# Clustered attention before a mixture of experts: the first head pair prepared on its own, v's scale taken per batch on ScalarE, and four transposes issued from ScalarE's queue

## The chip, the cores and the metric

The kernel runs on one core of a Trainium2 chip. The metric is the device time of one execution in microseconds. The kernel before took 1464.55 us (median of 3 runs, 1462.3 to 1464.61). The profile is that of one further execution, of 1462.42 us, whose span from the first to the last instruction is 1460.6 us.

## The reference

Only the attention part is touched by the change; the two dense stages behind it use its result.

```python
# q, k, v: (2, 8, 768, 64); centroids: (8, 16, 64)
q_assign = argmax(q_n . c_n);  k_assign = argmax(k_n . c_n)      # 16 clusters per head
mask = q_assign[:, :, :, None] == k_assign[:, :, None, :]
scores = where(mask, scale * q @ k.T, -1e9)
attn = softmax(scores)                                           # minus the row's maximum
x = attn @ v                                                     # (2, 8, 768, 64) -> (1536, 512)
h = x @ w_in;  x = (h * clip(h + 3, 0, 6) / 6) @ w_out            # d_ff 2048
# then 8 experts, each relu(x @ w1[e]) @ w2[e], weighted by a normalised gate
```

## The kernel before

The 16 heads of the two batches are worked as 8 pairs of heads, pair p holding heads 2p and 2p+1. A head has 6 tiles of 128 rows, so there are 96 units (head i, tile c), numbered g = 0 to 95. All engines run in the order in which the program writes the instructions; a wait on one of them holds up everything behind it on the same engine.

**Preparing a pair** (`prep_tasks`). ScalarE sums the squares of q and k (`squares`, L491). TensorE and VectorE turn the sums into power-of-two scales (`scale0` to `scale2`). Then `chain` splits q and k into two halves of 16 bits each: `hi` on ScalarE (L549), `lo` (L553) and `dup` (L560) on VectorE, and a DMA transpose gives qB and kB (L563). `sims` (L573, L574) compares them with the centroids on TensorE, five VectorE steps (`arg_max` to `arg_oh`) make the cluster codes, `rows` writes the codes beside the halves on ScalarE (L602, L603), and two more DMA transposes give qA and kA (L607). The last tasks are `vhi` (ScalarE, L530) and `vlo` (VectorE, L535), which split v with v's scale, and `abs1` to `abs3`. Pair 0 goes through `chain` in two parts, h0 and h1, one for each head, so that its first unit can start on the first half; the other pairs go through it in one (pair 1: `both1`).

**A unit.** `max_unit` multiplies 128 rows of q with all k (L680) and VectorE takes the maximum of each row (L683); it runs LEAD = 8 units ahead, so the loop starts at g = -8. `max_rows` writes the six maxima of a head into qA's rows and transposes them once more (L694). `s_mm` makes the scores on TensorE (L729, L733) and ScalarE takes the exponential E (L737). `e_split` splits E into Eh (ScalarE, L745) and El (L747 on VectorE for some units, L750 on GpSimd for the others). `pv_mm`, LAG = 4 units later, multiplies with v (L765). `evac_tasks` divides by the sums.

**v's scale.** Before, `scan_v` takes the largest modulus of v in four VectorE reductions of half a batch each (L836), and one scale serves both batches (`scale_v0`, `scale_v1`).

**What sets the order.** Ahead of the loop the order is written out by `go(...)`. Inside it, tasks are hung on units with `at(g, f)`: PLAN2 for pair 2, PLANV for the scans, v's scale and the last tasks of pairs 0 and 1. All DMAs, the transposes among them, are issued from SyncE's queue, in order. First weights of the dense stages are scanned and decoded between the units (L350, L181).

In the text "h0" and "h1" are pair 0's two halves, and E_4 is the exponential of unit g = 4.

Of the kernel before, what the change touches and what calls it, by code (L numbers as in the profile page):

```python
# [8 lines left out]
F32 = mybir.dt.float32  # L9
# [10 lines left out]
P = 128  # L20
NJ = 6
# [11 lines left out]
def attention_moe_kernel(  # L33
# [446 lines left out]
    def prep_tasks(p, parts=None):  # L480
# [46 lines left out]

        def vhi():
            vn = d["vn"] = ap3.tile([P, 2 * NJ, 130], F16, tag="vn", name=f"vn{p}")
            nc.scalar.activation(vn[:, :, 0:D], vr, AF.Copy, scale=sv[0][:, 0:1])  # L530
            nc.gpsimd.memset(vn[:, :, D:D + 1], 1.0)

        def vlo():
            vn = d["vn"]
            nc.vector.scalar_tensor_tensor(  # L535
                out=vn[:, :, D + 1:2 * D + 1], in0=vr, scalar=sv[0][:, 0:1], in1=vn[:, :, 0:D],
                op0=ALU.mult, op1=ALU.subtract)

        def chain(tr):
# [60 lines left out]
            def rows():  # L600
                oh = x["oh"]
                nc.scalar.activation(qa[:, tr, D:D + C], oh[:, 0:n], AF.Copy, scale=MASK)  # L602
                nc.scalar.activation(ka[:, tr, D:D + C], oh[:, n:], AF.Copy, scale=MASK, bias=-MASK)  # L603
                for nm, nat in (("q", qa), ("k", ka)):
                    if tr.start == 0:
                        d[nm + "A"] = ap2.tile([P, 2 * NJ, P], F16, tag=f"{nm}A", name=f"{nm}A{p}")
                    nc.sync.dma_start_transpose(  # L607
                        out=d[nm + "A"][:, tr], in_=nat[:, tr].rearrange("p a b -> p (a b)"))

            two = [lambda g=g, nm=nm: g(nm) for g in (hi, lo, dup) for nm in "qk"]  # L610
# [171 lines left out]
    def evac_tasks(i):  # L782
        p, hh = divmod(i, 2)
        b, hp = divmod(p, H // 2)
        ps = pvt.pop(i)
        if hh == 0:
            xn[p] = [ap2.tile([P, NJ, P], F16, tag=f"xn{z}", name=f"xn{z}_{p}") for z in range(2)]
        xs = xn[p]
        r = small.tile([P, NJ], F32, tag="x_r", name=f"x_r{i}")
        xf = ap2.tile([P, NJ, D], F32, tag="x_f", name=f"x_f{i}", bufs=1)  # L790
        xh, xl = (x[:, :, D * hh:D * hh + D] for x in xs)

        def e0():
# [83 lines left out]
    sv = [None, None]

    vred = []

    def scale_v0():
        nc.vector.tensor_reduce(pad[:, 0:1], vmx, axis=AX.X, op=ALU.max)
        vred.append(ps_v.tile([P, 2 * P], F32, tag="v", name="red_v"))
        red_rows(vred[0][:, 0:P])

    def scale_v1():
        to_all(red_max(vred[0][:, 0:P], "v"), vred[0][:, P:P + 1])
        sv[:] = scale_of(vred[0][:, P:P + 1], 1, 1, "v", const)
# [41 lines left out]
    def at(g, f):  # L930
        tasks.setdefault(g, []).append(f)
# [16 lines left out]

    for n, f in zip((2, 7, 9, 13, 14, 18, 19, 25, 26, 33, 35, 36, 47, 48), wscan):
# [877 lines left out]
```

## Time and profile before

| | |
|---|---|
| median of 3 runs | 1464.55 us (1462.3 to 1464.61) |
| the profiled execution / its span | 1462.42 us / 1460.6 us |
| TensorE busy | 1353.3 us, 93% |
| VectorE busy | 1200.2 us, 82% |
| ScalarE busy | 921.3 us, 63% |
| GpSimd busy | 795.6 us, 54% |

The attention part ends at about 300 us of the span; from there on TensorE is busy without a gap. The change lies in its first 70 us, where no engine is busy throughout and the engines wait for each other in turn. The way to read it is therefore not by busy shares but in order of time, engine by engine: which instruction waits there, for whom, and what stands behind it.

### The profile page before, as it was taken

The numbers are of one execution on the slowest core, as the hardware profiler recorded it, in microseconds if no ns is written. First come the engines' busy times: TensorE is split into PE (matmuls) and PEld (weight loads), VectorE is DVE, ScalarE is ACT, GpSimd is POOL, SyncE is SP. The second block draws the span as 40 slices with busy tenths as digits, with TensorE's granted clock in tenths as the row PEclk, the third lists the DMA queues.
The fourth block names the chain that finished last, engine by engine and source line by source line (L and its number), as shares of the span: only waits on it lengthen the run. The fifth ranks groups of instructions, "written<-read, shape, count | busy, mean of one in ns | idle before, by whom it ended". The sixth has DMA issues, their size and how long they took to land.

```text
span 1460.6 us, 31114 instructions
## 1 busy us (share of the span) xinstructions
PE 1353.3 (93%) x12334; PEld 1058.4 (72%) x12334; DVE 1200.2 (82%) x2111; ACT 921.3 (63%) x1723; POOL 795.6 (54%) x831
## 2 busy tenths in 40 slices
PE   2788777899999996989999999999999999999998
PEld 1456555644444445878888888888888888888887
DVE  8889998777775668788988988988988988988954
ACT  2679877867374456566767666666666656657642
POOL 1357866735034556365666566566566556656631
PEclk9889989999999998999999999999999999999999
DMA  8576644241312101101111111111111111111001
GB/s 223 127 170 115 140 99 68 53 127 59 126 65 59 45 17 31 31 32 31 45 31 46 44 31 46 44 31 45 44 32 45 45 31 46 45 31 46 8 31 51
DMA packets 150194, 88.92 MB, mean 61 GB/s; under 512 B 83488, under 2 KB 145952, under 8 KB 150048
## 3 DMA queue, kind: packets, MB, share of 16 engines
q1 hardware_dynamic: 150048, 86.94, 22.8%
q8 instruction: 96, 1.57, 0.5%
q14 instruction: 50, 0.41, 0.1%
HBM read 64.01 MB, written 3.15 MB: 46 GB/s over the span
## 4 chain that ended last, share of the span: by engine, by line
PE 67%; DVE 16%; ACT 7%; issue 5%; POOL 1%; DMA 1%; SPq 0%; DVEq 0%; ACTq 0%; POOLq 0%
PE o_X L1640 17%; PE X L1698 17%; PE o_Z L1640 9%; PE Z L1698 8%; PE Y L1698 4%; PE o_Y L1640 4%; DVE pmt L683 3%; PE l L1271 2%; ACT E L737 1%; DVE w_t L208 1%; DVE raw L210 1%; ACT Eh L745 1%; ACT u L1241 1%; PE l L921 1%; PE pmt L680 1%
## 5 line engine op out<-in xcount | busy, mean ns | idle before, releaser
L1698 PEld LDWEIGHTS <-wop 128*128 128x128 f16 x4032 | 395.5, 98 | 68.0 <-issue 20.9
L1640 PEld LDWEIGHTS <-g 128*128 128x128 f16 x4032 | 394.6, 98 | 45.5
L1640 PE MATMUL o_X<-ws,g 128*128 128x256 f16 x2304 | 311.9, 273 | 0.0
L1608 POOL TENSOR_TENSOR xT<-xT 128x256 f32<-128x256 f32 x96 | 79.2, 825 | 284.2 <-ACT xT L1709 273.4
L1604 DVE TENSOR_TENSOR g<-xT,g 128x512 f16<-128x512 f32 (+1 forms) x288 | 229.4, 797 | 0.1
L1698 PE MATMUL X<-xop,wop 128*128 128x256 f16 x1536 | 210.1, 274 | 17.3 <-ACT xT L1703 11.2
L750 POOL TENSOR_TENSOR El<-E,Eh 128x384 f16<-128x384 f32 x138 | 134.2, 997 | 118.9 <-ACT Eh L745 78.2
L1599 ACT CAST g<-xT 128x512 f16<-128x512 f32 (+1 forms) x288 | 157.8, 548 | 1.1 <-POOL xT L1612 1.1
L1703 ACT COPY xT<-X 128x256 f32<-128x256 f32 x192 | 71.3, 371 | 137.6 <-PE X L1698 137.3
L1640 PE MATMUL o_Z<-ws,g 128*128 128x256 f16 x1152 | 156.1, 273 | 0.0
L737 ACT ACTIVATE E<-pS,esc 128x768 f32<-128x768 f32 x96 | 86.3, 899 | 48.8 <-PE pS L733 47.7
L1249 POOL TENSOR_TENSOR hl<-u,hh 128x512 f16<-128x512 f32 x48 | 59.5, 1240 | 100.8 <-ACT hh L1248 100.8
L1709 ACT ACTIVATE xT<-xT 128x256 f32<-128x256 f32 x192 | 100.1, 521 | 13.9 <-DVE xT L1706 13.3
L1709 ACT ACTIVATE xT<-X 128x256 f32<-128x256 f32 x96 | 36.8, 383 | 111.9 <-PE X L1698 111.6
L1698 PE MATMUL Z<-xop,wop 128*128 128x256 f16 x768 | 105.9, 275 | 0.0
L1698 PE MATMUL X<-xT,wop 128*128 128x256 f16 x768 | 104.7, 273 | 0.5 <-DVE xT L1706 0.5
L1668 DVE SCALAR_TENSOR_TENSOR acc<-o_X,coef,acc 128x256 f32<-128x256 f32 x168 | 73.0, 475 | 28.1 <-PE o_X L1640 28.1
L1613 POOL TENSOR_TENSOR sb<-xT 128x256 f32<-128x256 f32 x96 | 91.7, 955 | 7.5
L1612 POOL TENSOR_TENSOR xT<-xT 128x256 f32<-128x256 f32 x96 | 92.5, 963 | 0.0
L683 DVE TENSOR_REDUCE pmt<-pmt 128x1 f32<-128x768 f32 x84 | 80.6, 959 | 14.4 <-PE pmt L680 13.8
L680 PE MATMUL pmt<-kA,qA 80*128 80x384 f16 x184 | 51.3, 365 | 43.3 <-DVE pmt L683 20.1
L1609 POOL TENSOR_TENSOR sb<-xT 128x256 f32<-128x256 f32 x96 | 84.6, 881 | 6.5 <-ACT xT L1703 4.3
(291 smaller groups left out, 2935.9 us busy)
## 6 DMA issues: line engine op xcount, KB each, us to landing
raw<-in_moe_w_dram SPq DMA_DIRECT2D x64, 256.0 KB, 3.2
raw<-in_moe_w_dram SPq DMA_DIRECT2D x32, 512.0 KB, 3.5
w_c<-in_moe_w_out_dram SPq DMA_DIRECT2D x16, 512.0 KB, 3.4
w00x<-in_moe_w_in_dram SPq DMA_DIRECT2D x8, 512.0 KB, 4.9
w00f<-in_moe_w_in_dram SPq DMA_DIRECT2D x8, 512.0 KB, 4.1
w_c<-in_moe_w_in_dram SPq DMA_DIRECT2D x8, 512.0 KB, 4.0
qraw<-in_q_dram SPq DMA_DIRECT2D x8, 384.0 KB, 3.7
kraw<-in_k_dram SPq DMA_DIRECT2D x8, 384.0 KB, 4.7
```

The lines of the kernel that those rows point to most:

```text
L683: nc.vector.tensor_reduce(nmx[i][:, j:j + 1], ps[:, :, 0:N2], axis=AX.XY, op=ALU.max, negate=True)
L737: nc.scalar.activation(E, ps[:, :, 0:N2], AF.Exp, scale=d["esc"][:, 0:1])
L750: nc.gpsimd.tensor_tensor(out=El[:, g], in0=E[:, g], in1=Eh[:, g], op=ALU.subtract)
L1599: nc.scalar.copy(t[:, 0] if n == 2 else t[:, 0, 0], src)
L1604: nc.vector.tensor_tensor(o, d[g], x, op=ALU.subtract)
L1608: nc.gpsimd.tensor_tensor(out=sa[:, 1], in0=q2, in1=q0, op=ALU.add)
L1609: nc.gpsimd.tensor_tensor(out=d["sb"][:, 0], in0=q3, in1=q2, op=ALU.subtract)
L1612: nc.gpsimd.tensor_tensor(out=sa[:, 0], in0=sa[:, 1], in1=q3, op=ALU.subtract)
L1613: nc.gpsimd.tensor_tensor(out=d["sb"][:, 1], in0=q1, in1=sa[:, 0], op=ALU.subtract)
L1640: nc.tensor.matmul(o, lhsT=x, rhs=r, start=first and z == 0, stop=last and z == 2, skip_group_check=True)
L1698: nc.tensor.matmul(o[n][:, 0:XT], lhsT=l, rhs=r, start=(first and c == 0 and z == 0), stop=(c == 1 and z == 2), skip_group_check=True)
L1709: nc.scalar.activation(q, q if src is None else src, AF.Relu)
```

## The change

Ahead of the loop, pair 0 now goes through squares, scale, split, transposes, similarities, codes and code rows before anything of pair 1 but its two squares is done. Pair 1's scale follows pair 0's codes, and its `chain` moves into the units g = -3 to 2. Pair 0's four transposes of k (kB and kA, h0 and h1) are issued from ScalarE's queue; those of q stay on SyncE's. v's scale is made per batch: `scan_v` is now one ScalarE activation per head, which takes the moduli and adds them up along the row; eight of them stand ahead of the loop, the other eight at units 1 to 4, two at a time. `scale_v(0)` stands at g = -1 and 0, `scale_v(1)` at g = 4 and 5; the factor between the two batches' scales is multiplied in `evac_tasks`, in the instruction that was there. El of units 0, 3 and 5 moves from VectorE to GpSimd.

```diff
-                nc.sync.dma_start_transpose(
+                (nc.scalar if (p, nm) == (0, "k") else nc.sync).dma_start_transpose(
                     out=d[nm + "B"][:, tr], in_=nB[:, tr].rearrange("p a b -> p (a b)"))
...
-                    nc.sync.dma_start_transpose(
+                    (nc.scalar if (p, nm) == (0, "k") else nc.sync).dma_start_transpose(
                         out=d[nm + "A"][:, tr], in_=nat[:, tr].rearrange("p a b -> p (a b)"))
...
-        if n % 12 in (0, 3, 5) or n >= NU - LEAD and n % 2:
+        if n % 12 in (0, 3, 5) and n > 5 or n >= NU - LEAD and n % 2:
...
     def scan_v(n):
-        b, z = divmod(n, 2)
-        nc.vector.tensor_reduce(
-            vmx[:, n:n + 1], vraw[b][:, 4 * z:4 * z + 4], axis=AX.XYZ, op=ALU.max, apply_absolute_value=True)
+        b, h = divmod(n, H)
+        junk = ap2.tile([P, NJ, D], F32, tag="x_f", name=f"v_t{n}", bufs=1)
+        nc.scalar.activation(junk, vraw[b][:, h], AF.Abs, accum_out=vmx[:, n:n + 1])
...
-    go(first0, 0, 1, 2)
-    go(first1, 0)
-    go(first0, 3)
+    go(first0, 0, 1, 2, 3)
     c3()
     go(first0, 4)
...
     go(h0, 0, 1)
-    go(first1, 1, 2)
+    go(h1, 0, 1)
     go(h0, 2, 4, 3, 5)
-    go(h1, 0, 1, 2, 4, 3, 5)
-    go(first1, 3, 4)
-    go(both1, 0, 1, 2, 4, 3, 5)
+    go(h1, 2, 4, 3, 5)
+    go(first1, 0, 1)
...
     go(h0, *range(6, 13))
     go(h1, *range(6, 13))
+    go(first1, 2, 3, 4)
     load_qk(2)
     load_v(1)
-    scan_v(0)
-    scan_v(1)
+    for n in range(H):
+        scan_v(n)
...
-    for f in both1[6:]:
-        at(-3, f)
-    for n, f in zip(PLANV, [lambda: scan_v(2), lambda: scan_v(3), scale_v0, scale_v1] + last0 + last1):
+    for n, f in zip((-3, -3, -3, -3, -2, -2, 0, 1, 1, 1, 1, 1, 2), both1):
+        at(n, f)
+    for n, f in zip((-1, 0, 0, 1, 3, 4, 4), scale_v(0) + tuple(last0)):
+        at(n, f)
+    for n, f in zip((5, 6, 6, 7, 7), last1):
+        at(n, f)
+    for n in range(H):
+        at(1 + n // 2, lambda n=n: scan_v(H + n))
+    for n, f in zip((4, 5, 5), scale_v(1) + (scale_x,)):
         at(n, f)
```

SyncE's queue before, from the centroids' transpose on. In these rows a name's last number tells the buffer, the digit ahead of it the pair (qB0 is pair 0's); the DMAHW semaphores are eight that the DMAs take in turn, in the program's order (the centroids' load has 0, CT 6, the first qB0 7, the next transpose 0).

```order
L471 DMA_TRANSPOSE CT_100<-ct_106 128x3x128 [waits DVE_49,Pool_49]
L563 DMA_TRANSPOSE qB0_183<-qnB0_151 128x6x128 [waits DVE_49,Activation_49]
L563 DMA_TRANSPOSE kB0_187<-knB0_153 128x6x128 [waits DMAHW0_49,DVE_49,Activation_49]
L563 DMA_TRANSPOSE qB0_183<-qnB0_151 128x6x128 [waits DMAHW1_49,DVE_49]
L563 DMA_TRANSPOSE kB0_187<-knB0_153 128x6x128 [waits DMAHW2_49,DVE_49]
L563 DMA_TRANSPOSE qB1_210<-qnB1_157 128x12x128 [waits DMAHW3_49,DVE_49,Activation_49]
L563 DMA_TRANSPOSE kB1_214<-knB1_177 128x12x128 [waits DMAHW4_49,DVE_49,Activation_49]
L607 DMA_TRANSPOSE qA0_254<-qnA0_93 128x6x128 [waits DMAHW5_49,Activation_49]
L607 DMA_TRANSPOSE kA0_256<-knA0_96 128x6x128 [waits DMAHW6_49,Activation_49,Pool_49]
```

Each waits for the engine that made its source and for the last user of its own semaphore. The same place of SyncE's queue in the changed kernel:

```order
L471 DMA_TRANSPOSE CT_100<-ct_106 128x3x128 [waits DVE_49,Pool_49]
L563 DMA_TRANSPOSE qB0_179<-qnB0_151 128x6x128 [waits DVE_49,Activation_49]
L563 DMA_TRANSPOSE qB0_179<-qnB0_151 128x6x128 [waits DMAHW1_49,DMAHW0_49,DVE_49]
L607 DMA_TRANSPOSE qA0_233<-qnA0_93 128x6x128 [waits DMAHW3_49,DMAHW2_49,Activation_49]
L607 DMA_TRANSPOSE qA0_233<-qnA0_93 128x6x128 [waits DMAHW5_49,DMAHW4_49,Activation_49]
L431 DMA qraw2_286<-in_q_dram 128x2x384 [waits DMAHW7_49]
```

The k transposes and pair 1's are gone from here, and each transpose that stays, but the first, waits for one semaphore more. ScalarE's queue in the changed kernel, from pair 0's last split on (the rows v_t are `scan_v`):

```order
L549 ACTIVATE knA0_96<-kraw0_117,qk_s0_166 128x6x64
L563 DMA_TRANSPOSE kB0_183<-knB0_153 128x6x128 [waits DMAHW6_49,DMAHW0_49,DMAHW7_49,DVE_49,Activation_49]
L563 DMA_TRANSPOSE kB0_183<-knB0_153 128x6x128 [waits DMAHW1_49,DVE_49]
L491 ACTIVATE qnB1_191,pad_70<-qraw1_119 128x768 [waits DMAHW3_49,PE_49]
L491 ACTIVATE knB1_193,pad_70<-kraw1_121 128x768 [waits DMAHW4_49]
L602 ACTIVATE qnA0_93<-a_oh0_229 128x6x16 [waits DVE_49,Pool_49]
L603 ACTIVATE knA0_96<-a_oh0_229 128x6x16 [waits Pool_49]
L607 DMA_TRANSPOSE kA0_235<-knA0_96 128x6x128 [waits DMAHW3_49,Activation_49,Pool_49]
L602 ACTIVATE qnA0_93<-a_oh0_269 128x6x16 [waits DVE_49]
L603 ACTIVATE knA0_96<-a_oh0_269 128x6x16
L607 DMA_TRANSPOSE kA0_235<-knA0_96 128x6x128 [waits DMAHW5_49,Activation_49]
L838 ACTIVATE v_t0_291,vmx_124<-vraw0_102 128x384
```

Seven more rows like the last follow, and then pair 1's `hi`; in the kernel before no DMA stands in this queue. On VectorE the changed kernel has this after the six maxima of unit -8 to -3:

```order
L697 TENSOR_SCALAR qnA0_93<-nmx0_307 128x6 [waits DMAHW3_49,DVE_49,Pool_49]
L698 SCALAR_TENSOR_TENSOR qnA0_93<-nmx0_307,qnA0_93 128x6 [waits DVE_49]
L553 SCALAR_TENSOR_TENSOR qnB1_191<-qraw1_119,qk_s1_280,qnA1_94 128x12x64 [waits Activation_49]
L553 SCALAR_TENSOR_TENSOR knB1_193<-kraw1_121,qk_s1_280,knA1_97 128x12x64 [waits DMAHW4_49,Activation_49]
L683 TENSOR_REDUCE nmx1_337<-pmt_101 128x1 [waits PE_49]
L560 COPY qnB1_191<-qnA1_94 128x12x64
L560 COPY knB1_193<-knA1_97 128x12x64
L683 TENSOR_REDUCE nmx1_337<-pm1_1_351 128x1 [waits PE_49]
L883 TENSOR_REDUCE pad_70<-vmx_124 128x1
```

Before, pair 1's two `lo` and `dup` stood ahead of pair 0's codes, and its five code steps stood here.

## Rows read from the trace of the kernel before

**Rows 1.** Windows: busy us and count of PE, PEld, DVE, ACT, POOL; granted clock.

```profile
61.00:75.00 14.00, 11.49 (x93) 7.43 (x91) 11.75 (x25) 7.07 (x9) 8.37 (x9) 0.52 0.70 155
82.00:92.00 10.00, 7.94 (x63) 5.47 (x63) 7.15 (x10) 5.51 (x9) 5.47 (x7) 0.50 0.59 110
100.00:125.00 25.00, 20.10 (x302) 14.61 (x301) 22.67 (x44) 21.58 (x30) 19.23 (x21) 1.00 0.71 151
320.00:340.00 20.00, 20.00 (x95) 9.07 (x93) 16.11 (x27) 16.10 (x30) 12.42 (x9) 1.00 0.23 78
```

**Rows 2.** Timeline of SyncE's queue: start us, us, issue; idle before and releaser.

```profile
12.13 1.21 SPq L563 DMA_TRANSPOSE qB<-qnB  x1
13.44 1.23 SPq L563 DMA_TRANSPOSE kB<-knB  x1
...
19.76 1.91 SPq L563 DMA_TRANSPOSE kB<-knB  x1
```

**Rows 3.** Issue to landing: L563 in 0 to 60 us.

```profile
DMA to landing us min/median/max: 2.8/2.8/4.3
```

**Rows 4.** Issue to landing: L607 in 36 to 40 us, pair 1's two.

```profile
DMA to landing us min/median/max: 3.8/3.9/4.0
```

**Rows 5.** Timeline of TensorE: first products, first scores, v's scale.

```profile
26.91 0.80 PE L680 MATMUL pmt<-kA,qA 80*128 80x384 f16 x2 [7.44 <-DMA kA<-knA]
...
38.90 0.84 PE L729 MATMUL pS<-qB,kB 128*128 128x384 f16 x2
...
45.48 0.45 PE L78 MATMUL red_v<-ident,pad 128*128 128x128 f32 x1 [3.18 <-DVE pad L882]
...
48.90 0.57 PE L88 MATMUL red_v<-ident,v_r 128*128 128x1 f32 x2
```

**Rows 6.** Timeline of VectorE, 17 to 93 us.

```profile
17.03 1.02 DVE L553 SCALAR_TENSOR_TENSOR qnB<-qraw,qk_s,qnA 128x768 f16<-128x768 f32 x1 [0.81 <-ACT qnA L549]
17.97 0.35 DVE L560 COPY qnB<-qnA 128x768 f16<-128x768 f16 x1
...
27.74 0.96 DVE L683 TENSOR_REDUCE nmx<-pmt 128x1 f32<-128x768 f32 x1 [0.76 <-PE pmt L680]
...
32.31 0.95 DVE L683 TENSOR_REDUCE nmx<-pm 128x1 f32<-128x768 f32 x1
...
40.01 1.74 DVE L836 TENSOR_REDUCE vmx<-vraw 128x1 f32<-128x1536 f32 x1
...
49.50 0.16 DVE L142 TENSOR_SCALAR v_e<-red_v 128x1 int32<-128x1 int32 x1 [0.91 <-PE red_v L88]
...
54.93 0.96 DVE L747 TENSOR_TENSOR El<-E,Eh 128x768 f16<-128x768 f32 x1 [1.19 <-ACT Eh L745]
...
92.17 0.97 DVE L683 TENSOR_REDUCE pmt<-pmt 128x1 f32<-128x768 f32 x1 [2.66 <-PE pmt L680]
```

**Rows 7.** Timeline of ScalarE, 36 to 55 us.

```profile
36.50 0.36 ACT L602 ACTIVATE qnA<-a_oh 128x192 f16<-128x192 f16 x1 [12.35 <-DVE a_oh L598]
...
40.42 0.90 ACT L737 ACTIVATE E<-pS,esc 128x768 f32<-128x768 f32 x1 [2.48 <-PE pS L733]
...
50.07 0.94 ACT L530 ACTIVATE vn<-vraw,v_s 128x768 f16<-128x768 f32 x1 [1.28 <-DVE v_s L147]
50.91 0.83 ACT L491 ACTIVATE qnB<-qraw 128x768 f16<-128x768 f32 x1
...
51.74 0.82 ACT L745 CAST Eh<-E 128x768 f16<-128x768 f32 x1
52.46 0.89 ACT L737 ACTIVATE E<-pS,esc 128x768 f32<-128x768 f32 x1
53.25 0.92 ACT L530 ACTIVATE vn<-vraw,v_s 128x768 f16<-128x768 f32 x1
...
54.80 0.89 ACT L737 ACTIVATE E<-pS,esc 128x768 f32<-128x768 f32 x1
```

**Rows 8.** ScalarE's groups over the whole span: count | busy us, mean ns.

```profile
L802 ACT CAST xn<-x_f 128x384 f16<-128x384 f32 x16 | 8.0, 501 | 1.2 <-DVE x_f L797 1.2
...
L262 ACT ACTIVATION_READ_ACCUMULATOR w_t<-raw 128x1 f32 x16 | 3.0, 187 | 0.0
```

More of the change, by code (lines that the diff above doesn't have):

```diff
@@ L529, in vhi @@
             vn = d["vn"] = ap3.tile([P, 2 * NJ, 130], F16, tag="vn", name=f"vn{p}")
-            nc.scalar.activation(vn[:, :, 0:D], vr, AF.Copy, scale=sv[0][:, 0:1])
+            nc.scalar.activation(vn[:, :, 0:D], vr, AF.Copy, scale=sb[b][0][:, 0:1])
             nc.gpsimd.memset(vn[:, :, D:D + 1], 1.0)
@@ L535, in vlo @@
             nc.vector.scalar_tensor_tensor(
-                out=vn[:, :, D + 1:2 * D + 1], in0=vr, scalar=sv[0][:, 0:1], in1=vn[:, :, 0:D],
+                out=vn[:, :, D + 1:2 * D + 1], in0=vr, scalar=sb[b][0][:, 0:1], in1=vn[:, :, 0:D],
                 op0=ALU.mult, op1=ALU.subtract)
@@ L794, in e0 @@
             return [
-                lambda: nc.vector.tensor_scalar(out=r, in0=ps[:, :, D], scalar1=1e-9, scalar2=None, op0=ALU.add),
+                lambda: nc.vector.tensor_scalar(
+                    out=r, in0=ps[:, :, D], scalar1=1e-9, scalar2=xb[b], op0=ALU.add, op1=ALU.mult),
                 lambda: nc.vector.reciprocal(r, r),
@@ L831, in attention_moe_kernel @@
     load_v(0)
-    vmx = small.tile([P, 4], F32, name="vmx")
+    vmx = small.tile([P, NHEAD], F32, name="vmx")
     def scan_v(n):
-        b, z = divmod(n, 2)
-        nc.vector.tensor_reduce(
-            vmx[:, n:n + 1], vraw[b][:, 4 * z:4 * z + 4], axis=AX.XYZ, op=ALU.max, apply_absolute_value=True)
+        b, h = divmod(n, H)
+        junk = ap2.tile([P, NJ, D], F32, tag="x_f", name=f"v_t{n}", bufs=1)
+        nc.scalar.activation(junk, vraw[b][:, h], AF.Abs, accum_out=vmx[:, n:n + 1])
     for t in (qnA[0], knA[0], qnA[1], knA[1], qnA[2]):
@@ L871, in attention_moe_kernel, with scale_v, a, c @@
     go(h1, *range(6, 13))
+    go(first1, 2, 3, 4)
     load_qk(2)
     load_v(1)
-    scan_v(0)
-    scan_v(1)
+    for n in range(H):
+        scan_v(n)
     sv = [None, None]
[L879 to L888, printed above, removed]
+    sb, xb = {}, {}
+    def scale_v(b):
+        d = {}
+        def a():
+            nc.vector.tensor_reduce(pad[:, 3:4], vmx[:, H * b:H * b + H], axis=AX.X, op=ALU.max)
+            d["red"] = ps_v.tile([P, 2 * P], F32, tag="v", name=f"red_v{b}")
+            red_rows(d["red"][:, 0:P])
+        def c():
+            ps = d.pop("red")
+            to_all(red_max(ps[:, 0:P], f"v{b}"), ps[:, P:P + 1], col=3)
+            sb[b] = scale_of(ps[:, P:P + 1], 1, 7, f"v{b}", ap1)
+        return a, c
+    def scale_x():
+        t = const.tile([P, 4], F32, name="sx")
+        for z, op in enumerate((ALU.min, ALU.max)):
+            sv[z] = t[:, z:z + 1]
+            nc.vector.tensor_tensor(sv[z], sb[0][z], sb[1][z], op=op)
+        for b in range(B):
+            xb[b] = t[:, 2 + b:3 + b]
+            nc.vector.tensor_tensor(xb[b], sb[b][0], sv[1], op=ALU.mult)
     NB = NT // 4
@@ L938, in attention_moe_kernel @@
     PLAN2 = [-1, 1, 2, 2, 3, 4, 5, 6, 6, 7, 7, 11, 11, 12, 12, 12, 13, 13, 5, 9, 14, 15, 15]
-    PLANV = [0, 1, 1, 2, 2, 3, 4, 5, 5, 3, 5, 6, 7, 7]
     plan(2, PLAN2)
```

## The prediction

> **What bounds the kernel now.** I read the windows first, then the timelines of SyncE, TensorE, VectorE and ScalarE side by side from 10 to 95 us. In the dense part TensorE is busy 20.00 of 20 us [rows 1]: what attention loses or wins arrives at the end undiminished, since nothing there has slack to give. In attention's steady part (100 to 125 us) VectorE comes nearest to a bound, 22.67 of 25 us, with ScalarE at 21.58 behind it. The change sits ahead of that, where a chain decides. The first product waits 7.44 us for kA and starts at 26.91 [rows 5]; E_0 starts at 40.42 and E_4 at 54.80, E_0 after a wait for its scores [rows 7]. Three stations carry my sum: the first product, E_0 and E_4.
>
> **The change part by part.** Up to the first qB the order is as before, so that is issued at 12.13 again [rows 2].
>
> *The transposes.* Before, all were on one queue, 1.31 us from start to start (12.13, 13.44) though each lands 2.8 us after its issue [rows 2, 3]: they overlap. In the new order q's and k's alternate between two queues, and by the waits printed there each waits for the semaphore of the one before it: kB h0 for 7 (qB h0), qB h1 for 0 (kB h0), kB h1 for 1 (qB h1), and so on to kA h1. So 2.8 us take the place of 1.31: qB h0 lands at 14.9, kB h0 at 17.7, qB h1 at 20.5, kB h1 at 23.3. ScalarE stands still meanwhile; it issues kB h1 at 20.5, is held 1.2 us by it if that costs what it costs SyncE [rows 2], does pair 1's two squares (0.83 each, 50.91 to 51.74 [rows 7]) and half a row of codes (0.3; the whole takes 0.36 [rows 7]), until 23.7. qA h0 is issued then, lands at 26.5, kA h0 at 29.3. The first product starts at 29.3, **2.4 us later** than before. VectorE's codes are done well inside these waits and cost nothing; if the waits were not there, they would be next.
>
> The row shows overlapping transposes on one queue and has none on two. The Trainium skill (DMA: Bandwidth & Descriptors, "Silent corruption: two transposing streams in flight at once") says that the later stream must wait for the earlier one's full completion; it speaks against splitting transposes over two queues, it has no time in it, and the printed waits agree with it.
>
> *ScalarE ahead of the loop.* kA h0's issue holds it to 27.7; qA h1 is issued at 29.3 and lands at 32.1; kA h1's issue lasts to 33.3. Behind it stand eight sums of moduli. The nearest rows are a 128x384 cast (0.50) and the read of a sum (0.19) [rows 8]; each sum waits for the one before because of a shared scratch tile, so I take 0.63, with ends 0.50 and 0.69. Eight are 5.0 us: 38.4. Only then comes pair 1's hi, 0.84: 39.2. VectorE has by then done its six maxima: they started 0.83 after the product and took 5.5 us to the end of the sixth (27.74, 32.31 plus 0.95 [rows 6]), so 35.7, and two small steps 0.6: 36.3. Pair 1's lo is next in its queue and waits for that hi: **3.0 us idle**. Behind it stand pair 1's lo and dup, the maxima of units -2, -1 and 0, and v's scale.
>
> *To E_0.* From 39.2: two lo (0.94 each, 17.03 to 17.97), two dup (0.27), two maxima (0.9 each) and v's step into pad, 0.2, make 43.7 [rows 6]. TensorE: 0.6 for red_v with its start, 0.64 for a pair of products, 1.28 for the four of the scores (0.64 from pair to pair, 38.90 to 39.54) [rows 5], 0.1 to start: E_0 at 46.3 against 40.42, **5.9 later**.
>
> *From E_0 to E_4*, 14.4 us before. Taken from VectorE: two scans of 1.74 (40.01) and El of unit 0, 0.96 [rows 6]; v's scale stood behind the scans, so these are real savings. But pair 1's similarities now stand between the scores and v's scale on TensorE. Its kB is issued at 43.9, and wide transposes beside loads land after 3.8 to 4.0 us [rows 4]: 47.8. Then 0.6 for the similarities of k, 0.6 for red_v's L88 [rows 5], three small steps of 0.2 (49.50 [rows 6]): v's scale at 49.6. ScalarE, by start-to-start steps of rows 7: vhi 0.84, Eh_0 0.72, E_1 0.79, a square 0.83, two sums 1.26, Eh_1 0.72, E_2 0.79: 55.6. Now q's code row, 0.36, qA of pair 1 at 56.0, kA 1.45 later, landing 3.9 on: 61.3. Unit 4's maximum needs it and stands ahead of unit 4's scores on TensorE: 0.64 + 1.28: E_4 at 63.3 against 54.80, **8.5 later**. Before, kA of pair 1 was there long ahead.
>
> *After E_4.* Added: two sums on ScalarE (1.3) and the second batch's scale on VectorE (nine small steps, 1.6). Taken: El of units 3 (its wait of 1.19 with it) and 5, 0.96 each [rows 6]. GpSimd has room for them. I take the balance, -0.2, as nothing. The factor in the evacuation rides in an instruction that was there. Loads, PLAN2 and the weights' scans stand at the same units and move along.
>
> Sum: 8.5 us on the profiled execution's 1462.42: 1470.9. That execution lies 2.1 under the median of the runs but beside the lowest of them (1462.3), so I forecast **1471 us**.
>
> Bounds. Low: ScalarE's issue costs nothing, the sums 0.50, pair 1's transposes land in 2.8: first product at 28.9, E_0 at 43.5, E_4 at 58.1 (+3.3). TensorE's granted clock was 0.52 in 61 to 75 us and 0.50 in 82 to 92, the lower of its levels of 1.2 and 2.4 GHz; VectorE idled there 2.25 and 2.85 us [rows 1]. If those stretches come at full clock in the new order, up to 5.1 comes back: 1460.6. High: half of the eight chained landings take 3.9 instead of 2.8, or two more such stretches come at half clock: some 5 more, 1476 to 1477.
>
> **The rivals.**
>
> *A. The delay sinks.* VectorE's idle time from E_4 to 95 us is the waiting for others (2.66 at 92.17 [rows 6], 5.1 in the two half-clock windows [rows 1]). If everything else stands ready by the time it arrives late, VectorE runs through and gives back about 7 of 8.5 us: 1464, no change. It decides if ScalarE and TensorE can run ahead of VectorE. Against it: both take their work in the order of the units, with two score banks, so they are late with it.
>
> *B. The change does what it says (faster).* The queues work side by side, with no transpose waiting for another's landing. kB h0 is issued at 12.8, kB h1 at 14.0; the first half's codes are written at 18.3 and kA h0 lands at 21.4: the first product comes 5.5 earlier, ScalarE's sums end before VectorE's maxima do, and E_0 is at about 35. E_0 to E_4 still grows, by 2.6. Gain 2.9: 1459.5. It decides from the point where kA h0 lands before 24 us. For it: 26.91 was a wait for a DMA. Against it: the printed waits, and no engine here ever passes a wait of its own.
>
> The Trainium skill's "Issuing engines are not separate DMA queues" (DMA: Bandwidth & Descriptors) would make even that small: a second issuing engine saves only the issuing. No run here shows transposes on two queues.
>
> *C. Slower still.* Landings of 3.9 us all along the chain: eight times 1.1 more, partly behind ScalarE's own work; or ScalarE becomes the bound from E_2 to E_8, where squares, splits, exponentials and sums, by the steps of rows 7, put some 19 us on it. 1478 or more. Against it: 2.8 is the median of the early ones [rows 3].
>
> **How the numbers follow.** Forecast (both waits bite) 0.60; A 0.15; B 0.11; C 0.14. About 0.2%, 2.9 us, is what a measurement can tell from no change. Faster is B, 0.11; same is A, 0.15; slower is the forecast and C, 0.74. The forecast's own range is 1466 to 1477; for 8 in 10 it has to reach over A: 1461 to 1477, leaving out most of B and of C.
>
> **What would show it.** In the changed profile: transposes of L563 and L607 2.8 us apart, alternating between SyncE's and ScalarE's queue, with ScalarE idle until some 22 us but for the splits; the first L680 at 29, not 21; eight sums of 0.6 on ScalarE between 33 and 39 with VectorE idle at 36 to 39, released by ScalarE's L549; E_0 near 46, E_4 near 63 after a wait for kA of pair 1. From 100 us on every line should lie some 8 us later than before, and the dense part should be as long as it was. The forecast is wrong if the first L680 comes before 27 us, if the sums end before the maxima, or if the shift between the two traces shrinks from E_4 to 100 us by more than half.

## The result and the profile after

The changed kernel takes 1482.32 us (median of 4 runs, 1481.53 to 1483.26) against 1463.58 us (the three runs from before and a fourth, 1462.61); the ratio is 1.0129, 95% interval 1.0116 to 1.0141. The forecast was 1471: slower, as forecast, but by 18.7 us instead of 8.5, and outside the range of 1461 to 1477. The profiled execution took 1481.73 us, its span is 1479.9 us.

The chain of waits of the changed kernel, in order of time (start us, us, what), begins with the transposes of pair 0:

```profile
10.69 3.48 DMA qB<-qnB
14.26 2.83 DMA kB<-knB
17.15 2.74 DMA qB<-qnB
...
23.26 2.77 DMA qA<-qnA
26.14 2.75 DMA kA<-knA
28.94 2.75 DMA qA<-qnA
31.77 9.15 DMA kA<-knA
```

q's and k's transposes alternate, one landing after the other, where two starts lay 1.31 us apart before [rows 2]. The last one, the second half's kA, lands after 9.15 us, at 40.92. The timeline of ScalarE (start us, us, instruction, idle before it and releaser) shows what stands behind:

```profile
31.77 1.32 ACTq L607 DMA_TRANSPOSE kA<-knA  x1
33.14 0.52 ACT L838 ACTIVATE v_t<-vraw 128x384 f32<-128x384 f32 x1 [5.27 <-issue]
...
38.19 0.92 ACT L549 ACTIVATE qnA<-qraw,qk_s 128x768 f16<-128x768 f32 x1
...
46.86 0.90 ACT L737 ACTIVATE E<-pS,esc 128x768 f32<-128x768 f32 x1 [6.10 <-PE pS L733]
...
58.11 0.90 ACT L737 ACTIVATE E<-pS,esc 128x768 f32<-128x768 f32 x1 [0.88 <-PE pS L733]
58.91 0.35 ACT L602 ACTIVATE qnA<-a_oh 128x192 f16<-128x192 f16 x1
...
67.16 0.90 ACT L737 ACTIVATE E<-pS,esc 128x768 f32<-128x768 f32 x1 [2.27 <-PE pS L733]
...
73.15 0.90 ACT L737 ACTIVATE E<-pS,esc 128x768 f32<-128x768 f32 x1 [2.40 <-PE pS L733]
...
82.72 0.90 ACT L737 ACTIVATE E<-pS,esc 128x768 f32<-128x768 f32 x1 [2.98 <-PE pS L733]
```

The L737 rows are E_0, E_2, E_4, E_5 and E_7. VectorE and TensorE in the same stretch, in two timelines:

```profile
35.59 0.19 DVE L698 SCALAR_TENSOR_TENSOR qnA<-nmx,qnA 128x6 f16<-128x6 f32 x1
39.15 1.02 DVE L553 SCALAR_TENSOR_TENSOR qnB<-qraw,qk_s,qnA 128x768 f16<-128x768 f32 x1 [3.37 <-ACT qnA L549]
...
70.06 0.16 DVE L883 TENSOR_REDUCE pad<-vmx 128x1 f32<-128x8 f32 x1 [1.68 <-ACT v_t L838]
```

```profile
28.93 0.80 PE L680 MATMUL pmt<-kA,qA 80*128 80x384 f16 x2 [2.74 <-DMA kA<-knA]
...
41.05 0.80 PE L680 MATMUL pmt<-kA,qA 80*128 80x384 f16 x2 [6.99 <-DMA kA<-knA]
...
70.68 0.45 PE L78 MATMUL red_v<-ident,pad 128*128 128x128 f32 x1 [2.64 <-DVE Wt L641]
...
79.22 1.48 PE L621 MATMUL abs<-vn,knA 128*128 128x129 f16 x12 [1.88 <-DVE vn L535]
```

and SyncE's queue:

```profile
40.98 1.21 SPq L694 DMA_TRANSPOSE qA<-qnA  x1
...
43.42 2.92 SPq L563 DMA_TRANSPOSE qB<-qnB  x1
46.39 1.54 SPq L563 DMA_TRANSPOSE kB<-knB  x1
```

L694 transposes the first head's maxima. VectorE had them ready at 35.78; the transpose is issued at 40.98, 0.06 us after the second half's kA has landed: here too a transpose of one queue goes out only when the open one of the other has landed. The Trainium skill (DMA: Bandwidth & Descriptors, "Silent corruption: two transposing streams in flight at once") asks for that wait; the trace agrees, here and in the chain above.

From E_0 on I compare starts of the exponentials. Against the kernel before E_0 comes 6.4 us later, E_4 12.4, E_8 17.8, unit 24's 18.0 and unit 95's 18.0. Nearly all of the loss is made in the first nine units. In the dense part TensorE is as busy as before; the span is 19.3 us longer, and the 1.3 us that come in behind unit 95 were not followed (window rows: PE, PEld, DVE, ACT, POOL busy us and count, granted clock):

```profile
61.00:75.00 14.00, 8.88 (x67) 6.09 (x66) 5.30 (x21) 9.27 (x19) 5.49 (x8) 1.00 0.59 139
...
320.00:340.00 20.00, 20.00 (x94) 9.06 (x93) 15.06 (x26) 13.94 (x26) 8.19 (x6) 1.00 0.38 137
```

One caution on these lags. In the profile of the kernel before, VectorE's first instruction took 4.56 us; in the changed kernel it took 0.58, and in no other kernel of this document more than 1.26. Before, then changed:

```profile
1.19 4.56 DVE L853 TENSOR_SCALAR ident<-ident 128x128 f32<-128x128 int32 x1 [0.33 <-POOL ident L819]
```

```profile
1.19 0.58 DVE L854 TENSOR_SCALAR ident<-ident 128x128 f32<-128x128 int32 x1 [0.33 <-POOL ident L820]
```

The first qB was issued at 12.13 there, at 10.69 in the changed kernel and between 10.16 and 11.04 in the other kernels below. So the first lags may be up to 1.4 us too small; how much of this reaches E_0 was not tested.

### The profile page after: what moved, and what is told of

Read it like the earlier page. It is cut to its first block, busy times and chain, and to the rows that moved or that the text cites. A ratio compares the mean times of both kernels' runs of the same rounds, so it can differ in the third digit from the quotient of the medians.

```text
span 1479.9 us, 31159 instructions
## 1 busy us (share of the span) xinstructions
PE 1358.1 (92%) x12337; PEld 1060.6 (72%) x12337; DVE 1185.1 (80%) x2114; ACT 931.1 (63%) x1755; POOL 797.2 (54%) x837
## 4 chain that ended last, share of the span: by engine, by line
PE 71%; DVE 14%; ACT 5%; issue 4%; DMA 4%; POOL 2%; SPq 0%; ACTq 0%; DVEq 0%; POOLq 0%
PE o_X L1658 17%; PE X L1716 17%; PE o_Z L1658 9%; PE Z L1716 8%; PE Y L1716 4%; PE o_Y L1658 4%; DVE pmt L683 3%; PE l L934 2%; PE l L936 2%; PE l L935 2%; PE l L1289 2%; PE pv L765 1%; PE pmt L680 1%; DMA kA<-knA 1%; PE pS L733 1%
## 5 line engine op out<-in xcount | busy, mean ns | idle before, releaser
L750 POOL TENSOR_TENSOR El<-E,Eh 128x384 f16<-128x384 f32 x144 | 139.0, 990 | 131.1 <-ACT Eh L745 84.7
L737 ACT ACTIVATE E<-pS,esc 128x768 f32<-128x768 f32 x96 | 86.4, 900 | 55.0 <-PE pS L733 51.2
L680 PE MATMUL pmt<-kA,qA 80*128 80x384 f16 x184 | 52.1, 369 | 47.8 <-DVE pmt L683 17.9
```

The lines of the kernel that those rows point to most:

```text
L737: nc.scalar.activation(E, ps[:, :, 0:N2], AF.Exp, scale=d["esc"][:, 0:1])
```

## The experiments

In each expectation T is the theory and R its rival. The theory: the split queues cost what they cost at E_0, and behind E_0 it is pair 1's late chain and the second batch's scale. The rivals: the loss is made elsewhere and early gains only wait, or the waits named are covered by others. Each kernel was profiled once; the last four columns are the lags of its exponentials behind the kernel before (40.42, 54.80, 67.81 and 116.14 us), in us. The medians of the kernel before, measured beside them, are 1462.45 to 1464.02. E_0 of e2, whose edit lies behind E_4, is 1.7 us later than that of the changed kernel, so differences of 1 to 2 us between two profiles prove nothing alone.

| kernel | median us | ratio to before, 95% | E_0 | E_4 | E_8 | unit 24 |
|---|---|---|---|---|---|---|
| changed kernel | 1482.32 | 1.0129 (1.0116 to 1.0141) | +6.4 | +12.4 | +17.8 | +18.0 |
| e1: k on SyncE | 1471.03 | 1.0041 (1.0022 to 1.0059) | -3.6 | +0.6 | +5.3 | +5.2 |
| e4: before, k on ScalarE | 1475.22 | 1.0087 (1.0072 to 1.0102) | +11.9 | +11.8 | +11.4 | +12.1 |
| e5: before, v's part | 1466.57 | 1.0026 (1.0009 to 1.0042) | 0.0 | -2.0 | +2.4 | +1.4 |
| e6: before, order alone | 1469.03 | 1.0044 (1.0027 to 1.0061) | -4.6 | +5.7 | +6.4 | +6.6 |
| e3: hi first | 1479.89 | 1.0117 (1.0094 to 1.0140) | +5.6 | +10.6 | +15.4 | +16.1 |
| e7: loads late | 1483.14 | 1.0133 (1.0114 to 1.0153) | +5.9 | +15.1 | +19.4 | +18.1 |
| e8: hi first and loads late | 1485.48 | 1.0158 (1.0141 to 1.0174) | +5.7 | +14.2 | +18.8 | +17.5 |
| e13: hi first, last kA on SyncE | 1483.15 | 1.0130 (1.0113 to 1.0147) | +2.2 | +9.0 | +13.9 | +16.5 |
| e2: second scale late | 1483.49 | 1.0133 (1.0118 to 1.0148) | +8.1 | +14.1 | +17.0 | +19.9 |
| e9: e1, rows at unit 1 | 1466.95 | 1.0029 (1.0016 to 1.0041) | -4.0 | -1.4 | +2.8 | +1.6 |
| e10: e1, last tasks early | 1468.94 | 1.0048 (1.0031 to 1.0064) | -3.9 | +0.1 | +0.4 | +2.0 |
| e11: e1, last tasks, first scale, sims moved | 1467.83 | 1.0036 (1.0024 to 1.0047) | -2.4 | +1.0 | +2.9 | +3.0 |
| e12: e9 and e10 | 1467.90 | 1.0037 (1.0025 to 1.0049) | -5.1 | -0.8 | +1.1 | +1.2 |
| e14: e12, scales early | 1465.56 | 1.0020 (1.0009 to 1.0032) | -4.3 | +2.0 | -1.3 | +1.7 |
| e15: e12, second sums ahead | 1469.81 | 1.0047 (1.0035 to 1.0059) | -1.1 | +3.1 | -0.3 | +0.5 |
| e16: old order, second sums ahead | 1463.82 | 1.0007 (0.9995 to 1.0018) | +2.1 | +1.5 | -1.9 | +1.3 |

**The queues, taken back and alone.** e1 undoes the split at both lines, e4 makes it alone:

```diff
-                (nc.scalar if (p, nm) == (0, "k") else nc.sync).dma_start_transpose(
+                nc.sync.dma_start_transpose(
```

> The changed kernel with pair 0's four k transposes put back on SyncE's queue; everything else (order, sums of moduli on ScalarE, second scale) stays as changed. Theory T (the alternation between two queues costs 2.8 us a hop, and the last one, kA h1, got stuck behind the loads): the transposes come 1.3 us apart again, the first product falls from 28.9 to some 23, the second half's kA no longer lands at 40.9, ScalarE's eight sums end near 32 instead of 38, VectorE has no wait of 3.4 for pair 1's hi, E_0 is at some 37 to 39 instead of 46.9, and the time falls by 8 to 10 us, to 1472 to 1474. Rival R (the loss is made after E_0, by pair 1's late codes and the second batch's scale, and whatever comes earlier waits there): 1479 or more, with E_0 early and E_8 as late as in the changed kernel, 85.6.

> The kernel before with pair 0's four k transposes issued from ScalarE's queue and nothing else changed. Theory T (the prediction's term: q's and k's transposes wait for one another's landing, 2.8 us instead of 1.3, and ScalarE stands still behind them): the transposes alternate 2.8 us apart, E_0 comes 5 to 8 us later than 40.4 and the time is 1469 to 1472. Rival R (before, the first product stood behind pair 1's transposes and codes anyway, so the slower hops fill a wait that was there): E_0 later by 2 or less, the time 1466 or less.

In e1 SyncE's queue issues without waiting for a landing:

```profile
10.36 1.21 SPq L563 DMA_TRANSPOSE qB<-qnB  x1
11.68 1.63 SPq L563 DMA_TRANSPOSE kB<-knB  x1
...
22.15 1.24 SPq L607 DMA_TRANSPOSE kA<-knA  x1
...
30.13 1.22 SPq L694 DMA_TRANSPOSE qA<-qnA  x1
```

The first product starts at 23.26, E_0 at 36.83, 10.0 earlier, and 11 us of the time are gone; R's late E_8 did not come (73.15). Alone, the split costs 12.1 us at unit 24; on top of the rest it costs 18.0 - 5.2 = 12.8: it adds, undiminished. T's mechanism holds for both, but its numbers were too low: in e1 the time falls by 11.3 instead of 8 to 10, in e4 E_0 is 11.9 us late instead of 5 to 8 and the time 1475.22 instead of 1469 to 1472. In e4 pair 1's transposes stand in the same chain, so that the first product starts at 34.29 instead of 26.91, and there too the last transpose is stuck (chain of e4):

```profile
31.41 2.75 DMA kA<-knA
...
34.21 2.74 DMA qA<-qnA
...
37.05 11.13 DMA kA<-knA
```

But e1 is still slower than before: what is left of the change loses 5.2 us, though its E_0 comes 3.6 earlier.

**Who holds E_0.** Four kernels on the changed one ask which late arrival E_0 waits for (the "guests" of the expectations). e3:

```diff
+    go(both1, 0, 1)
     for n in range(H):
         scan_v(n)
...
-    for n, f in zip((-3, -3, -3, -3, -2, -2, 0, 1, 1, 1, 1, 1, 2), both1):
+    for n, f in zip((-3, -3, -2, -2, 0, 1, 1, 1, 1, 1, 2), both1[2:]):
```

> The changed kernel with pair 1's hi of q and k put ahead of the eight sums of moduli on ScalarE. Theory T (the prediction's step: VectorE's 3.4 us of idle time for that hi are on the path to E_0): E_0 3 us earlier, the time down by 3, to 1479. Rival R (the second half's kA, landed only at 40.9 behind the loads, holds unit -2's product and so E_0 anyway): E_0 moves by less than 0.7 and the time by 0.5 or less.

e7 (pair 2's tasks keep their places), and e8, which is e3 and e7:

```diff
-    load_qk(2)
-    load_v(1)
...
+    at(-2, lambda: load_qk(2))
+    at(-2, lambda: load_v(1))
```

> The changed kernel with the loads of pair 2's q and k and of the second batch's v issued at unit -2, behind the transposes of the first head's maxima, instead of ahead of the loop. Theory T (kA h1, issued at 31.8, landed after 9.2 us only since those three loads were in the way): it lands within 3 us, at 34.6, TensorE's wait of 7.0 us for it is gone, but VectorE's wait for pair 1's hi stays, so that E_0 comes 1 to 2 us earlier, and the time falls by 1 to 2, to 1480 to 1481. Rival R (the 9.2 us have another reason, a free buffer or a queue's own wait): kA h1 still lands 8 us or more after its issue and the time stays within 0.7 of 1482.

> The changed kernel with both edits that did little one by one: pair 1's hi ahead of the eight sums, and the three loads behind the transposes of the first head's maxima. Theory T (E_0 has two late guests of nearly the same lateness, VectorE's wait for hi and the second half's kA stuck behind the loads, so that only both together move it): E_0 at 43 to 44 instead of 46.9 and the time about 3 below the changed kernel, 1478 to 1480, if pair 1's transposes are not made later by the loads. Rival R (something third holds E_0): E_0 at 45.5 or later.

e13 is e3 with the second half's kA on SyncE's queue, ahead of the loads:

```diff
-                    (nc.scalar if (p, nm) == (0, "k") else nc.sync).dma_start_transpose(
+                    (nc.scalar if (p, nm, tr.start) == (0, "k", 0) else nc.sync).dma_start_transpose(
                         out=d[nm + "A"][:, tr], in_=nat[:, tr].rearrange("p a b -> p (a b)"))
```

> The changed kernel with pair 1's hi ahead of the eight sums and, of the four k transposes, the last one (kA of the second half) back on SyncE's queue, ahead of the three loads; the other three stay on ScalarE's. Theory T (two guests come equally late to E_0, VectorE's wait for hi and the second half's kA held up by the loads, with the transposes of the first maxima held behind it): kA h1 lands by 33.5, the transpose of the maxima is issued at 37.5 instead of 41.0, E_0 is at 42 to 43 instead of 46.9, the time falls by 4 to 5, to 1478. Rival R (something else holds E_0 at 46): E_0 at 45.5 or later, the time above 1480.

e3 moves E_0 by 0.8 and e7 by 0.6: neither is enough, and neither time can be told from that of the changed kernel (e3's runs are 1478.43 to 1485.56, e7's 1481.12 to 1486.00). What moved in e3 was the landing of the second half's kA (chain of e3, then of e2):

```profile
31.89 8.22 DMA kA<-knA
```

```profile
31.88 10.70 DMA kA<-knA
```

It lands at 40.92 in the changed kernel, 40.11 in e3 and 42.58 in e2, and E_0 follows 5.94 or 5.95 us behind it in all three: that landing holds E_0. In e7 kA's product waits 0.60 us instead of 6.99, in TensorE's and SyncE's timelines:

```profile
35.07 0.80 PE L680 MATMUL pmt<-kA,qA 80*128 80x384 f16 x2 [0.60 <-DMA kA<-knA]
```

```profile
36.21 1.21 SPq L694 DMA_TRANSPOSE qA<-qnA  x1
```

So the 9.15 us were the loads' doing, and L694 was held by that landing; but hi still comes behind the sums (VectorE waits 3.27 us for it), E_0 gains only the 0.6, and the time does not move. e8 came out as R has it, but by a side effect of its own edit, so it decides nothing on E_0: with the loads late pair 2's squares wait for them on ScalarE, and v's scale behind (TensorE idle 7.24 us at 43.72). e13 frees both guests and leaves the loads alone: E_0 at 42.58, as T said. Two late arrivals, 0.6 us apart, held E_0.

What T got wrong is the end: the 4.3 us are 4.0 at E_8, 1.6 at unit 24 and none in the time. In e13 the lead shrinks from unit 17 on, where TensorE waits for a transpose of maxima and its products take 0.80:

```profile
115.43 0.80 PE L733 MATMUL pS<-qA,kA 82*128 82x384 f16 x2 [1.30 <-DMA qA<-qnA]
```

The granted clock there is 0.77, in the changed kernel 1.00 (windows of e13, then of the changed kernel):

```profile
110.00:125.00 15.00, 12.89 (x175) 9.02 (x175) 11.45 (x18) 9.24 (x13) 7.52 (x9) 0.77 0.95 220
```

```profile
110.00:125.00 15.00, 11.46 (x205) 8.62 (x204) 13.77 (x27) 12.04 (x16) 8.37 (x10) 1.00 1.07 235
```

e15 and e16 lose their leads over the kernel before in the same units (0.9 and 1.3 us early at unit 16, 0.5 and 1.3 late at unit 24). Both take part: e13's lead over the changed kernel is 3.96 us at unit 17, 2.56 at unit 18, whose product waited 1.30 for the transpose, and 1.27 at unit 19, whose products take 0.83 to 0.86 instead of 0.48 to 0.54. Why the products slow down there was not tested.

**Order and v apart.** e6 takes from the change the order of the pairs alone (the lines of `go` and of `both1`), e5 v's part alone (`scan_v`, `scale_v`, `scale_x`, El, the last tasks).

> The kernel before (its order of the pairs, its queue) with v's scale per batch from ScalarE's sums of moduli alone, and El of units 0, 3 and 5 on GpSimd as in the changed kernel. Theory T (the second batch's scale, on TensorE ahead of unit 5's product, and the sixteen sums on ScalarE are what costs behind E_0): E_0 is early or as before, 38 to 40.5, E_8 is 4 us or more later than 67.8, and the time is 1467 to 1470. Rival R (this part frees VectorE of four scans and three El and costs nothing; what costs behind E_0 is pair 1's late preparation): 1460 to 1464.

> The kernel before with the order of the two pairs alone changed (pair 0 through its codes first, pair 1's chain at units -3 to 2); v's scans stay on VectorE, one scale, all transposes on SyncE. Theory T (pair 1's late chain, its transposes landing in 4 us, its similarities on TensorE ahead of v's scale and its codes in the tile of the products are what costs behind E_0): E_0 comes some 3 us earlier than 40.4, E_8 is 5 us or more later than 67.8, and the time is 1468 to 1472, as with the sums on ScalarE (1471). Rival R (the order is harmless by itself, the sums and the second scale cost): 1461 to 1465.

Each loses behind E_0. e6 is T: E_0 4.6 earlier, E_4 5.7 later, the time 1469.03. e5 lies at 1466.6, between its two expectations: at E_4 it is 2.0 ahead, then loses 4.4 to E_8. Together (e1, 5.2 at unit 24) they cost less than the sum, 8.0; and the three parts, 12.1, 1.4 and 6.6, make 20.1 against the 18.0 of the whole.

**The second scale.** e2 moves it, on the changed kernel:

```diff
-    for n, f in zip((4, 5, 5), scale_v(1) + (scale_x,)):
+    for n, f in zip((7, 8, 8), scale_v(1) + (scale_x,)):
```

> The changed kernel with the second batch's scale of v and the factor between the scales at units 7 and 8 instead of 4 and 5. Theory T (that scale's chain from ScalarE's sums over VectorE's pad and TensorE's red_v stands in front of unit 5's product and costs the part lost behind E_4, 1.7 + 2.6 + 1.3 us of waits between 68 and 73): E_5 comes 3 to 4 us earlier than 73.2 and the time falls by about 4, to 1478. Rival R (these waits hide under pair 1's hi, lo and similarities, which are as late without it): within 1.5 us of the changed kernel's 1482.

R. E_4 to E_5 falls from 6.0 to 3.5 us, but E_7 to E_8 grows from 2.9 to 5.6 and E_8 to E_9 from 2.5 to 6.7. The scale goes VectorE, TensorE, VectorE, TensorE, VectorE, and each time it stands in these engines' queues ahead of the next unit's product or maximum; moved, it waits elsewhere.

**Pair 1's chain and last tasks.** On e1; e9 changes the last number, e10 two of five:

```diff
-    for n, f in zip((-3, -3, -3, -3, -2, -2, 0, 1, 1, 1, 1, 1, 2), both1):
+    for n, f in zip((-3, -3, -3, -3, -2, -2, 0, 1, 1, 1, 1, 1, 1), both1):
...
-    for n, f in zip((5, 6, 6, 7, 7), last1):
+    for n, f in zip((3, 5, 6, 7, 7), last1):
```

> All transposes on SyncE as in the 1471 us run, and pair 1's code rows on ScalarE at unit 1 instead of 2, so that they do not stand behind E_2. Theory T (the chain through pair 1's kA sets E_4): rows done 2.5 us earlier, kA issued at 47.6 instead of 50.05, E_4 at 53 instead of 55.4, the time 2 to 2.5 below 1471. Rival R (E_4 to E_8 is set by VectorE's and TensorE's work, and waits grow there by what E_4 wins): E_8 unchanged at 73.2, the time within 1 of 1471.

> All transposes on SyncE as in the 1471 us run, and the last tasks of pair 1 (vhi, vlo, abs) at units 3, 5, 6, 7, 7 as they were before the change, instead of 5, 6, 6, 7, 7. Theory T (TensorE's abs products wait 3.3 us for vlo, which the change moved to the same unit, and unit 7's product stands behind them): that wait goes, E_7 comes 2 to 3 us earlier than 70.8, the time is 1468.5 to 1469.5. Rival R (E_8 waits for VectorE anyway): E_8 unchanged at 73.2, the time within 1 of 1471.

> All transposes on SyncE, with both edits that helped one by one: pair 1's code rows at unit 1 and pair 1's last tasks at units 3, 5, 6, 7, 7. Theory T (the two losses lie one behind the other, before and after E_4, so they add): E_4 at 53, E_8 at 66 to 67, 1464 to 1466, no slower than the kernel before by more than 0.2%. Rival R (both ease the same wait of VectorE): 1467 or more.

In e9 ScalarE writes the code rows ahead of E_2 and E_4 comes at 53.36:

```profile
44.79 0.36 ACT L602 ACTIVATE qnA<-a_oh 128x192 f16<-128x192 f16 x1 [0.68 <-DVE a_oh L598]
...
53.36 0.89 ACT L737 ACTIVATE E<-pS,esc 128x768 f32<-128x768 f32 x1
```

At unit 24 3.6 us are won and the median falls by 4.1, more than T gave, though the runs overlap (1467.46 to 1471.79 in e1, 1466.10 to 1471.09 in e9). In e10 TensorE's wait for vlo (3.26 at 67.27 in e1) is gone:

```profile
63.61 0.86 PE L621 MATMUL abs<-vn,knA 128*128 128x129 f16 x12
```

E_7 comes 4.2 us earlier than in e1: T, as far as the wait goes. The median falls by 2.1, as T said, but that lies inside the spread of e10's own runs (1465.63 to 1471.29). The two do not add: e12 leads e9 by 0.5 us at unit 24 and its time is no lower. R there.

e11 moves similarities, codes and rows behind unit 1's scores (both1 from its seventh task on at unit 1) and the first scale to units -5 and -4, with e10's edit.

> All transposes on SyncE, pair 1's last tasks at units 3, 5, 6, 7, 7, and in addition the first batch's scale of v at units -5 and -4 (its eight sums are done by 25.5) and pair 1's similarities, codes and code rows at unit 1, behind unit 1's scores. Theory T (everything that is late behind E_0 is the chain similarities, scale, codes, rows, kA of pair 1 and the tasks packed behind it): E_0 stays at 37, E_1 follows within 3 us instead of 6, E_4 is at 51.5 to 53, E_8 at 66 to 68, and the time is 1459 to 1464, the level of the kernel before or a little better. Rival R (the loss behind E_0 is mere work on VectorE and ScalarE that had to be done somewhere): E_8 at 71 or later, the time 1468 or more.

Neither theory's numbers: E_1 follows E_0 in 2.3 us as T said, but VectorE then waits 3.50 us for pair 1's similarities and TensorE 3.00 for its codes, and E_2 comes at 48.85, later than in e1.

e14 adds to e12 the first scale at -5 and -4 and the second sums at units 1 and 2; e15 and e16 put those sums at -2 and -1 and the second scale at 0 and 1, e15 on e12, e16 on e5 with e10's edit:

```diff
-        at(1 + n // 2, lambda n=n: scan_v(H + n))
+        at(-2 + n // 4, lambda n=n: scan_v(H + n))
-    for n, f in zip((4, 5, 5), scale_v(1) + (scale_x,)):
+    for n, f in zip((0, 1, 1), scale_v(1) + (scale_x,)):
```

> As the kernel with rows and last tasks moved, and in addition the first batch's scale at units -5 and -4 and the second batch's eight sums at units 1 and 2, four at a time, instead of 1 to 4. Theory T (E_4 to E_5 takes 6 us since the second scale's first step waits for the last two sums, which stand behind E_4 on ScalarE): E_4 to E_5 falls to 4.5 or less, and the time is 1 to 2.5 us below the kernel without these two edits. Rival R (the round trip VectorE, TensorE, VectorE, TensorE of that scale costs the same wherever its sums stand): E_4 to E_5 stays at 5.5 to 6 and the time within 0.7.

> All transposes on SyncE, rows at unit 1, last tasks at 3, 5, 6, 7, 7, and the second batch's eight sums at units -2 and -1, its scale and the factor at units 0 and 1. Theory T (the second scale is what is left of the loss): E_4 to E_5 falls from 6 to 2.4, unit 24 comes 1 to 3 us before that of the kernel before, 1461 to 1464. Rival R (the rest is pair 1's late chain, and its waits grow by what the scale gives): unit 24 still 0 to 1.5 us later than before, the time 1465 or more.

> The kernel before in its order of the pairs and with all transposes on SyncE, with v's scale per batch from ScalarE's sums as in the changed kernel, but the second batch's eight sums at units -2 and -1, its scale and the factor at units 0 and 1, and pair 1's last tasks at 3, 5, 6, 7, 7. Theory T (sixteen sums on an idle ScalarE in place of four scans of 1.74 us on VectorE are a gain as long as nobody waits for the second scale): E_4 2 us earlier than 54.8, E_8 at 65 to 66.5, the time 1 to 3 us below the kernel before. Rival R (the scans lay in VectorE's waits): E_8 at 67 or later, the time the same as before or above.

In e14 E_4 to E_5 takes 2.3 us instead of 6.0, as before the change (54.80 to 57.14):

```profile
56.80 0.90 ACT L737 ACTIVATE E<-pS,esc 128x768 f32<-128x768 f32 x1
59.14 0.90 ACT L737 ACTIVATE E<-pS,esc 128x768 f32<-128x768 f32 x1
```

So that wait was the one for the sums: T. But E_4 itself comes 2.8 us later than in e12, with four sums at a time between E_1 and E_3, and at unit 24 nothing is won; the time is 2.3 us lower than e12's. In e15 E_4 to E_5 takes 2.3 us too, but ScalarE's second sums wait 6.41 us for the load of v (at 33.45), the scores stand behind, and E_0 comes 4.0 us later than in e12; E_8 is as early as before, and from unit 24 to 95 another 4.2 us are lost, which no run explains. Its time is R's. e16 reaches T's E_8 (65.94) but not T's time: it is level with the kernel before, the only one of the sixteen. None beats it.

## Why the prediction was wrong

**First product: right mechanism, and luck in the number.** The transposes alternate, with landings of 2.74 to 2.83 us behind the first and 1.23 to 1.32 per issue on ScalarE. That 28.93 lies so near the 29.3 worked out is luck: the chain started 1.44 us earlier than assumed (10.69 instead of 12.13) and took 18.24 us instead of 17.2, mostly since the first qB landed after 3.48 us instead of 2.8. Counted from the first qB, the first product came 3.5 us later than before, not 2.4.

**To E_0: one late arrival missed, and the same luck.** The eight sums take 0.65 each, VectorE waits 3.37 us for hi (3.0 forecast), E_0 is at 46.86 (46.3); counted from the first qB it is 7.9 us later than before, not 5.9. That the second half's kA would run behind the loads, which now go out just ahead of it from the other queue, and would hold L694, was not seen. It cost little there, because hi was as late.

**From E_0 to E_4: the term was too small**, 5.9 instead of 2.6 us. kB of pair 1 was to be issued at 43.9 and to land at 47.8; qB goes out ahead of it only at 43.42 and its issue holds SyncE 2.92 us, so kB goes out at 46.39 and lands at 50.19. v's scale and E_1 are some 2.4 us late with it. Then the product ahead of unit 2's scores waits for pair 1's codes, a wait that was not in the sum:

```profile
55.99 0.80 PE L680 MATMUL pmt<-kA,qA 80*128 80x384 f16 x2 [2.59 <-DVE a_oh L598]
```

E_2 and the code rows behind it (58.91) are 3.3 us late, kA is issued at 60.86 instead of 57.45: E_4 at 67.16, 3.9 late. That the rows stood behind E_2 was in the sum, but not that this place was worth 3.6 us at unit 24 (e9).

**After E_4: the step that failed.** "I take the balance, -0.2, as nothing" compared busy time: two sums and nine small steps against two El. What counts is what waits in order. E_4 to E_5 takes 6.0 us instead of 2.3, because the second scale's first step waits for the last two sums (1.68 us at 70.06) and red_v stands ahead of unit 5's product; E_6 to E_7 takes 4.8 instead of 1.8, because `vlo` of pair 1 was moved to the unit of the products that need it (79.22). With 0.8 more from E_5 to E_6 and 1.9 less from E_7 to E_8 that makes 18.5 us from E_4 to E_8 against 13.0: 5.5 us that had a price of nothing. That both waits were there is shown: in e14 the first is gone and E_4 to E_5 takes 2.3 us, in e10 the second and E_6 to E_7 takes 1.7, both on e1's transposes. How far the waits alone made the 5.5 us is not: the products ran slower too. Unit 5's after and before:

```profile
70.92 0.85 PE L680 MATMUL pmt<-kA,qA 80*128 80x384 f16 x2
71.56 0.85 PE L729 MATMUL pS<-qB,kB 128*128 128x384 f16 x2
```

```profile
55.07 0.49 PE L680 MATMUL pmt<-kA,qA 80*128 80x384 f16 x2
55.40 0.49 PE L729 MATMUL pS<-qB,kB 128*128 128x384 f16 x2
```

By these starts, 0.64 and 0.33 us apart, a unit's three pairs take an estimated 0.9 us longer, and no run separates this pace from the waits. The move of pair 1's last tasks stood in the diff and was not priced at all.

By its own stations the sum was 5.9 + 2.6 + 0; measured are 6.4 + 5.9 + 5.5, and 0.2 more up to unit 24. The rest was not followed.

**The rivals.** A: the lag from E_4 on did not shrink, it grew. B's mechanism is refuted by the chain; e1 shows that its price was wrong too: with the transposes close together E_0 comes early, as B said, and the kernel is still slower than before. C came nearest in its time, 1478 or more, but not for its reasons: six of the eight landings were at 2.8 (3.48 the first, 9.15 the last), and from E_2 to E_8 ScalarE had the work that C gave it, 18.57 us, but in 27.5 us, and waited for the others in between. The low bound hung on the granted clock of 61 to 75 us; it did come at 1.00 there, but the pairs of products took 0.80 to 0.85 us all the same, and VectorE, with 5.30 us of work in 14, stood waiting: nothing came back.

What stays open: how the 5.5 us divide between waits and the pace of the products, why an early start meets a late transpose and slow products at units 17 to 20, and the 1 to 4 us by which some profiles drift later between units 24 and 95.

## What to carry to other kernels

Do not put one chain of DMA transposes on two queues: here each then waited for the other's landing, and loads in flight beside one of them also held up the next one of the other queue. When a step is moved in an in-order schedule, price the waits at its new place, and read who stands behind it on every engine that it crosses; the balance of busy time says nothing there. A step that waits for two late arrivals moves only when both come earlier, and then look how far the lead travels before counting it.

## What was not expected of the hardware

A DMA transpose issued behind three loads of another queue landed 9.15 us after its issue (8.22 in e3, 10.70 in e2, 11.13 in e4), against under 2.9 us with the loads later (e7: issued at 32.17, its product at 35.07). And the granted clock of a stretch does not give the speed of the products in it: from 61 to 75 us it stands at 1.00 after and at 0.52 before, and a pair of L680 products after a wait takes 0.80 us in both (at 64.98 after, at 65.69 before).
